# Attention with scores, maxima and values in TensorE tiles of 64 rows by 32 columns

## The chip, the cores and the metric

The kernel runs on one core of one Trainium2 chip. The metric is the device time of one execution in microseconds (us); less is better. Engines are named as in the profile: PE is TensorE (matmuls; PEld its weight loads), DVE is VectorE, ACT is ScalarE, POOL is GpSimd, SP is SyncE, which issues most DMAs.

## The reference

A transformer block on one sequence of 2048 rows and 512 columns, in float32: layer norm, attention with 32 heads of 16 columns, an output projection and a residual, then layer norm, a feed-forward part of width 1792 with SiLU, and a residual.

```python
def _A_ref(x, wqkv, wo):
    qkv = (x @ wqkv) split into q, k, v      # 32 heads of 16 columns
    scores = einsum("bhqd,bhkd->bhqk", q, k) * 16 ** -0.5
    o = einsum("bhqk,bhkd->bhqd", softmax(scores), v)
    return o @ wo
def _B_ref(x, w1, w2):
    return silu(x @ w1) @ w2
h = x + _A_ref(layernorm(x), A_wqkv, A_wo)
return h + _B_ref(layernorm(h), B_w1, B_w2)
```

## The kernel before, in words

**Stages.** A prelude normalizes and transposes the rows and projects q, k and v. Then come 32 *items* of attention; an item is four heads (two pairs, `HEADS`, line 55) by one block of 512 queries, so that eight items make a query block. After each of the first three query blocks the feed-forward part of that block runs as a stage of its own (`finish_block`, line 1104; `mlp`, line 1041), in the middle of the loop over groups; the last one runs at the end (`finish_last`, line 1121).

**Groups.** An item has 16 *groups* of 128 keys; the loop over the 512 groups starts at line 1244. Each group does three things for TensorE:

- *Scores* (`scores`, line 451): for each of the four heads a matmul with 128 keys as the stationary operand and 512 queries moving, contraction over 64 rows (48 of data and 16 that carry the maximum of each query), float16. The two heads of a pair lie in rows 0 to 63 and 64 to 127 of `ks` and `qs` (`64 * j`), so that scores of different `j` use different halves of TensorE's rows. ScalarE takes the exponential of the 128 by 512 result from PSUM into a float32 tile `pt` (line 460).
- *Maxima* (`maximum`, line 273) of a later item: a matmul with 128 queries stationary and 512 keys moving, over 48 rows, and on VectorE a maximum over the 512 (line 289). `one_max` (line 393) picks one of the half that is asked for. How many a group does is set by `maxima` (line 1221) from what is due; in the attention stretches it is three in nearly every group and two in the third group of an item (`JOINT`, line 1236). More are done in the prelude and in the feed-forward stages.
- *Values* (`values`, line 815) of the group two before (`LAG`): four float32 matmuls over all 128 keys, one for each head, with the 17 columns of `va` (16 of v and one of ones) stationary and `pt` moving. Head `k` writes PSUM rows `32 * k` on, so that the four use four different quarters of TensorE's columns. They add up over the 16 groups of the item in one PSUM bank, `pv`.

**Order.** All engines run their work in the order in which the program states it (`keep_in_program_order`). In a group the four scores come in turn with the maxima, each maximum on the other half of the rows than the score before it (lines 1287 to 1300); then what else is due (transposed maxima of an item, `place_max`, line 326; output projection, `output`, line 1087); then the four value products (line 1312).

**Banks.** PSUM has eight banks of 128 by 512 float32. In attention, four serve the scores in turn (`st`), three the maxima (`sm`), one is `pv` (lines 802 to 804).

**Item's end.** After the item's last values, `finish_item` (line 833) copies `pv` into the tile `pvs` (VectorE; ScalarE for items 8, 16 and 24, `FIRSTS`), and DMAs carry sums and values on. The last item has its two head pairs one after the other, the first ended by `finish_part` (line 862). In items 8, 16 and 24 the last groups also hold the output projection and the layer norm of the query block before, whose products take banks from `st`.

Of the kernel before, what the change touches and what calls it, by code (L numbers as in the profile page):

```python
# [10 lines left out]
F32 = mybir.dt.float32  # L11
# [4 lines left out]
ALU = mybir.AluOpType  # L16
# [4 lines left out]
P = 128  # L21
# [4 lines left out]
DH = 16  # L26
# [4 lines left out]
KC = S // P  # L31
# [16 lines left out]
LAG = 2  # L48
# [40 lines left out]
def attention_mlp_kernel(ctx: ExitStack, tc: tile.TileContext, x, wqkv, wo, w1, w2, out):  # L89
    nc = tc.nc  # L90
    x = x.flatten_outer_dims()
# [3 lines left out]
    def mm(*a, **k):  # L95
        tc.keep_in_program_order(nc.tensor.matmul(*a, **k))  # L96
# [12 lines left out]
    def act(fn, *a, **k):  # L109
        pin(getattr(nc.scalar, fn)(*a, **k))  # L110

    def dve(fn, *a, **k):
        pin(getattr(nc.vector, fn)(*a, **k))  # L113
# [115 lines left out]
    ks, qs = [None] * RING, [None] * RING  # L229
# [3 lines left out]
    va = vpool.tile([P, KC, H, DH + 1], F32, name="va")  # L233
# [36 lines left out]

    mx, left = {}, {}

    def maximum(i, kb, qt, a, j, n):

        piece = piece_of(i, a)
        width = 1 if i == LAST else 2
        if piece not in mx:
            mx[piece] = small.tile([P, 64], F32, name="mx", bufs=RING + 1)[:, :32 * width].rearrange(
                "p (j a q k) -> p j a q k", j=2, a=width, k=4)
            left[piece] = 32 * width  # L280
        heads = (0, 1) if j is None else (j,)
        for m, h in enumerate(heads):
            mm(space[:, n + m, :], qs[i % RING][64 * h:64 * h + 48, a, qt * P:qt * P + P],
               ks[i % RING][64 * h:64 * h + 48, a, kb * 512:kb * 512 + 512], start=True, stop=True)
        of = mx[piece][:, :, a % width, qt, kb]
        if j is None:
            pin(nc.vector.tensor_reduce(of, space[:, n:n + 2, :], axis=AX.X, op=ALU.max))  # L287
        else:
            pin(nc.vector.tensor_reduce(of[:, j:j + 1], space[:, n, :], axis=AX.X, op=ALU.max))  # L289
# [59 lines left out]
    at = {"item": 0, "done": 0, "half": 0, "step": 0, "due": 0, "attention": False, "group": None, "ready": 0, "next": 0, "blocks": True}  # L349
    agenda, late = {}, {}  # L350

    def soon(steps, fn, *a):
# [459 lines left out]
    wo_l = cpool.tile([P, DC, D], F16, name="wo_l")  # L812
    hth = cpool.tile([P, DC, 512], F16, name="hth")
    htl = cpool.tile([P, DC, 512], F16, name="htl")
    def values(g):
        i, c = divmod(g, KC)
        n = KC if i < LAST else HALF
        for k in range(4):
            a, j, keys = head(g, k)
            mm(pv[32 * k:32 * k + DH + 1, :], va[:, keys, 4 * (i % 8) + 2 * a + j, :], pts.pop((g, k)),  # L820
               start=c % n == 0, stop=c % n == n - 1)
        if c == KC - 1:
            finish_item(i)
        elif c % n == n - 1:
            finish_part()

    def place(i, k):

# [1 line left out]
        r = (4 * i + 2 * a + j) % 8 * 16  # L830
        return slice(r, r + 16)

    def finish_item(i):

        b, u = divmod(i, 8)
        pvs = bp.tile([P, 512], F32, name="pvs", bufs=1)
        if i == LAST:
            act("copy", pvs[:, :256], pv[:, :256])
            dve("tensor_copy", pvs[:, 256:], pv[:, 256:])
        elif i in FIRSTS:  # L840
            act("copy", pvs, pv)
        else:
            dve("tensor_copy", pvs, pv)
        if i == LAST:
            last.append(pvs)
            return
        dma(dn[i], pvs.rearrange("(k r) n -> k r n", r=32)[:, DH, :])
        for k in range(4):
            dma(ot[b % 2][place(i, k), :, u // 2, :], pvs[32 * k:32 * k + 16, :].rearrange("d (t n) -> d t n", n=P))

        steps = (1, 4, 5, 7) if u == 7 else (2, 6, 8, 10)
        for n, fn in zip(steps, (sums, invert, spread, divide) if u % 2 else (sums, invert, spread)):
            soon(n, fn, i)
        if i == ITEMS - 2:
            soon(10, divide_half)
            soon(12, split_half)
# [2 lines left out]

    def finish_part():
        pvs = bp.tile([P, 512], F32, name="pvs", bufs=1)
        dve("tensor_copy", pvs, pv)
# [176 lines left out]
    def mlp(b):  # L1041
# [18 lines left out]
                singles(2)  # L1060

        gates = []
        lay_out(st=range(4))
        for f in range(FC):
            tick()
            next_weights()
# [37 lines left out]
    def finish_block(b, pending):  # L1104

        act("activation", small.tile([P, 1], F32, name="sw"), ident[:, :1], AF.Silu)
        load_weights("w1", 4)
        for g in pending:
            values(g)
        mlp(b)  # L1110

# [9 lines left out]
    def finish_last(pending):  # L1121
        b = NB - 1
        for g in pending:
            values(g)
# [119 lines left out]
    for g in range(groups):  # L1244
# [35 lines left out]
                    load_weights("w1", f)  # L1280
                load_weights("w2", 0)
        if g == 1:
            dve("memset", pv, 0.0)
        at["group"] = g
        n = maxima(g)

        half = 1 - head(g, g % 2)[1]
        j = next_item()
        more = len(todo[j, half]) - len(todo[j, 1 - half]) if j < ITEMS else 0
        beside = range(n)  # L1290
        if n == 3 and more < 0:
            beside = range(1, 4)
        if n == 2 and more > 0:
            beside = 0, 2
        for m in range(4):
            k = m ^ (g % 2)
            if (g, k) not in pts:
                scores(g, k)
            if m in beside:
                one_max(1 - head(g, k)[1])  # L1300
        if found_at["step"] < at["step"]:
            finish_rest()
        for j in late.pop(at["step"], ()):
# [43 lines left out]
```

## Time and profile before

| | |
|---|---|
| device time, median of 3 runs (lowest to highest) | 1611.66 us (1611.49 to 1613.15) |
| profiled execution: its own time | 1613.29 us |
| profiled execution: span of the records | 1611.5 us, 28300 instructions |
| granted TensorE clock | 1.0 |
| value products (`ps<-pt,va`) | 4096 matmul records, mean 598 ns |
| scores (`ps<-qs,ks`) | 2048, mean 379 ns |
| maxima (`ps<-ks,qs`) | 2048, mean 380 ns |
| exponentials (`pt<-ps` on ACT) | 2048, mean 631 ns |

A line of a group reads: line of the kernel, engine, operation, output and inputs by the program's names, shapes, count, then busy time in us, mean ns of one, and idle time of the engine just before them with what ended it. Of a matmul, `64*128` ahead of the shape is the part of the array that it uses: 64 rows by 128 columns. Instructions of one engine overlap in the records (a matmul's or an exponential's mean is longer than the distance to the next one), so the distance between starts tells the pace. A line of the view in order of time begins with start and length in us and ends with the count of instructions merged in it. A line of busy time by stretch has the stretch, its length, and for PE, PEld, DVE, ACT and POOL the busy us with the number of instructions, then clock, DMA share and GB/s. Nearly all matmuls carry line 96 and all VectorE operations but reductions line 113, those of helpers, so groups are told apart by tile names.

### The profile page before, as it was taken

The page shows a single profiled execution, that of the slowest core. Times are in us where ns is not written, and L with a number is a line of the kernel's source. Part 1 is how long each engine was busy: PE and PEld are TensorE (multiplying, and loading weights), DVE is VectorE, ACT ScalarE, POOL GpSimd, SP SyncE. Part 2 cuts the span into 40 slices and gives each one's busy share as a digit, 9 for nine tenths or more (in the row PEclk, how much of TensorE's full clock was granted, in tenths as well). Part 3 has the DMA queues.
Part 4 walks back from the last instruction along what each step waited for, and adds up shares of the span by engine and source line. Part 5 has one row for each costly group of instructions (what it writes and reads, how often), then busy time and mean ns, then how long its engine had stood idle before and what let it go on. Part 6 is the DMA issues. An engine that isn't in the chain of part 4 may idle for free.

```text
span 1611.5 us, 28300 instructions
## 1 busy us (share of the span) xinstructions
PE 1590.8 (99%) x10553; PEld 477.9 (30%) x10553; DVE 1392.9 (86%) x2060; ACT 1210.3 (75%) x2387; POOL 456.4 (28%) x702
## 2 busy tenths in 40 slices
PE   9999999999999999999999999999999999999998
PEld 6433222222233322222233322222233322222253
DVE  7899999999989889999989889999976789999421
ACT  6545799999964179999964179999964089999732
POOL 4743544544326101211136101211126101111100
PEclk9999999999999999999999999999999999999999
DMA  5668533342322111121223211121123111100222
GB/s 194 181 162 234 139 85 90 110 140 85 101 63 99 60 52 33 37 60 33 51 73 99 60 52 33 38 59 33 50 75 108 50 52 38 33 11 22 73 85 72
DMA packets 100949, 125.89 MB, mean 78 GB/s; under 512 B 24144, under 2 KB 61072, under 8 KB 100812
## 3 DMA queue, kind: packets, MB, share of 16 engines
q1 hardware_dynamic: 96204, 115.71, 25.1%
q10 hardware_dynamic: 4608, 8.39, 1.9%
q8 instruction: 82, 1.34, 0.3%
q14 instruction: 55, 0.45, 0.1%
HBM read 93.45 MB, written 24.63 MB: 73 GB/s over the span
## 4 chain that ended last, share of the span: by engine, by line
PE 85%; DVE 6%; ACT 4%; DMA 2%; issue 1%; POOL 1%; SPq 1%; DVEq 0%; ACTq 0%; POOLq 0%
PE ps L96 84%; ACT pt L110 4%; DVE mx L289 2%; DVE mx L287 2%; PE ps L99 1%; DMA qd<-sh 1%; DVE ot L113 1%; SPq L116 1%; DMA qs<-mt 0%; DVE st L113 0%; DMA ks<-in_A_x_dram 0%; DVE htl L113 0%; DVE hx L113 0%; POOL ri L103 0%; DVE pvs L113 0%
## 5 line engine op out<-in xcount | busy, mean ns | idle before, releaser
L110 ACT ACTIVATE pt<-ps 128x512 f32<-128x512 f32 x2048 | 1011.3, 631 | 154.9 <-PE ps L96 153.4
L289 DVE TENSOR_REDUCE mx<-ps 128x1 f32<-128x512 f32 x1474 | 926.8, 683 | 44.9 <-PE ps L96 16.1
L96 PE MATMUL ps<-qs,ks 64*128 64x512 f16 x2048 | 533.6, 379 | 5.8 <-DMA qs<-mt 2.5
L96 PE MATMUL ps<-pt,va 128*17 128x512 f32 x4096 | 537.5, 598 | 0.6
L96 PE MATMUL ps<-ks,qs 48*128 48x512 f16 x2048 | 494.7, 380 | 1.8 <-DVE mx L287 1.8
L287 DVE TENSOR_REDUCE mx<-ps 128x2 f32<-128x1024 f32 x287 | 334.0, 1219 | 55.1 <-PE ps L96 54.1
L96 PEld LDWEIGHTS <-ks 64*128 64x128 f16 x2048 | 150.8, 95 | 553.0 <-issue 433.2
L103 POOL TENSOR_TENSOR ri<-rc,minus 128x16 f32<-128x16 f32 x31 | 90.7, 2925 | 294.8 <-DMA rc<-dn 294.8
L96 PE MATMUL ps<-w,gh 128*128 128x512 f16 x672 | 157.4, 380 | 0.5 <-ACT g L110 0.4
L96 PEld LDWEIGHTS <-qs 48*128 48x128 f16 x2048 | 125.1, 94 | 75.3 <-issue 61.9
L96 PE MATMUL ps<-hth,w 128*128 128x512 f16 (+1 forms) x472 | 132.9, 369 | 0.0
L96 PEld LDWEIGHTS ps<-pt,va 128*17 128x17 f32 x4096 | 68.9, 95 | 214.6 <-issue 201.1
L110 ACT ACTIVATE g<-ps,factors 128x512 f32<-128x512 f32 x56 | 38.6, 689 | 124.6 <-PE ps L96 102.9
L96 PEld LDWEIGHTS <-w 128*128 128x128 f16 x708 | 66.1, 98 | 79.1 <-issue 11.8
L103 POOL TENSOR_TENSOR mx<-mx 128x32 f32<-128x32 f32 x36 | 8.6, 239 | 281.8 <-DVE mx L289 216.6
L96 PEld LDWEIGHTS <-gh 128*128 128x128 f16 x672 | 61.1, 98 | 85.5 <-issue 19.8
L96 PE MATMUL ps<-htl,w 128*128 128x512 f16 (+1 forms) x236 | 83.9, 368 | 0.0
L103 POOL TENSOR_SCALAR nm<-nm 128x16 f32<-128x16 f32 (+1 forms) x51 | 12.9, 254 | 169.8 <-DVE nm L303 154.5
L110 ACT ACTIVATE ks<-ps 128x512 f32<-128x512 f32 x30 | 18.0, 599 | 50.3 <-PE ps L96 37.6
L113 DVE SCALAR_TENSOR_TENSOR gh<-g,factors,gh 128x512 f16<-128x512 f32 x14 | 10.5, 751 | 52.2 <-ACT gh L110 52.2
L103 POOL TENSOR_TENSOR sl<-ks,sh 128x512 f16<-128x512 f32 x30 | 35.3, 1178 | 52.9 <-ACT sh L110 38.5
L103 POOL TENSOR_TENSOR gh<-g,gh 128x512 f16<-128x512 f32 x42 | 48.5, 1154 | 3.5
(153 smaller groups left out, 983.5 us busy)
## 6 DMA issues: line engine op xcount, KB each, us to landing
ks<-kd SPq DMA_DIRECT2D x120, 192.0 KB
w<-w1d SPq DMA_DIRECT2D x56, 256.0 KB
w<-w2d SPq DMA_DIRECT2D x56, 256.0 KB
ks<-in_B_w_dram ACTq DMA_DIRECT2D x28, 256.0 KB
w<-in_B_w_dram SPq DMA_DIRECT2D x28, 256.0 KB
qs<-qd SPq DMA_DIRECT2D x128, 48.0 KB
kd<-sh SPq DMA_DIRECT2D x16, 256.0 KB
qd<-sh SPq DMA_DIRECT2D x16, 256.0 KB
```

Of the source, the lines that this page charges most:

```text
L96: tc.keep_in_program_order(nc.tensor.matmul(*a, **k))
L99: tc.keep_in_program_order(nc.tensor.transpose(*a))
L103: tc.keep_in_program_order(getattr(nc.gpsimd, op)(*a, **k))
L110: pin(getattr(nc.scalar, fn)(*a, **k))
L113: pin(getattr(nc.vector, fn)(*a, **k))
L116: pin(nc.sync.dma_start(*a))
L287: pin(nc.vector.tensor_reduce(of, space[:, n:n + 2, :], axis=AX.X, op=ALU.max))
L289: pin(nc.vector.tensor_reduce(of[:, j:j + 1], space[:, n, :], axis=AX.X, op=ALU.max))
```

## The change

In attention every matmul of a group gets one tile shape, 64 rows by 32 columns:

- `narrow` issues a score or a maximum as four matmuls, one for each 32 columns of the stationary operand; each writes 32 rows of the same PSUM bank. It does so while `at["narrow"]` is set, which is in attention and not in the feed-forward stages.
- `values` is split by keys: half 0 takes keys 0 to 63, half 1 keys 64 to 127, each with four matmuls over 64 rows and with a PSUM bank of its own (banks 6 and 7).
- A group is written as two halves. In the first: a score of the heads in rows 64 to 127, values of half 0 (rows 0 to 63), then one or two maxima and the second score, all of rows 64 to 127. In the second the row halves are exchanged.
- The banks in attention are three for scores, three for maxima, two for values; the feed-forward stages have theirs as before.
- At an item's end `copy_values` copies half 0's bank into `pvs` and adds half 1's bank to it on VectorE.

By the program's order TensorE has 50,126 matmuls and weight loads in place of 21,102; the other engines' work is that of before but for the additions into `pvs`. The diff, cut to its core:

```diff
+    def narrow(ps, w, x):
+        for t in range(4) if at["narrow"] else (None,):
+            cols = slice(None) if t is None else slice(32 * t, 32 * t + 32)
+            mm(ps[cols, :], w[:, cols], x, start=True, stop=True)
...
-            mm(space[:, n + m, :], qs[i % RING][64 * h:64 * h + 48, a, qt * P:qt * P + P],
-               ks[i % RING][64 * h:64 * h + 48, a, kb * 512:kb * 512 + 512], start=True, stop=True)
+            narrow(space[:, n + m, :], qs[i % RING][64 * h:64 * h + 48, a, qt * P:qt * P + P],
+                   ks[i % RING][64 * h:64 * h + 48, a, kb * 512:kb * 512 + 512])
...
-        mm(ps, ks[i % RING][64 * j:64 * j + 64, a, c * P:(c + 1) * P], qs[i % RING][64 * j:64 * j + 64, a, :],
-           start=True, stop=True)
+        narrow(ps, ks[i % RING][64 * j:64 * j + 64, a, c * P:(c + 1) * P], qs[i % RING][64 * j:64 * j + 64, a, :])
...
-    idle_bank, last_bank = banks["st"]
-    lay_out(st=range(4), sm=(4, 5, last_bank))
-    pv = space[:, idle_bank, :]
+    def lay_out_attention():
+        lay_out(st=range(3), sm=range(3, 6))
+        at["narrow"] = True
+    lay_out_attention()
+    pv = [space[:, 6 + n, :] for n in range(2)]
...
-    def values(g):
+    def values(g, half):
         i, c = divmod(g, KC)
         n = KC if i < LAST else HALF
+        rows = slice(64 * half, 64 * half + 64)
         for k in range(4):
             a, j, keys = head(g, k)
-            mm(pv[32 * k:32 * k + DH + 1, :], va[:, keys, 4 * (i % 8) + 2 * a + j, :], pts.pop((g, k)),
+            pt = pts.pop((g, k)) if half else pts[g, k]
+            mm(pv[half][32 * k:32 * k + DH + 1, :], va[rows, keys, 4 * (i % 8) + 2 * a + j, :], pt[rows],
                start=c % n == 0, stop=c % n == n - 1)
-        if c == KC - 1:
-            finish_item(i)
-        elif c % n == n - 1:
-            finish_part()
+        if c % n == n - 1:
+            copy_values(i, c == KC - 1, half)
...
+    def copy_values(i, whole, half):
+        if not half:
+            pvs = bp.tile([P, 512], F32, name="pvs", bufs=1)
+            sums_of.append(pvs)
+            if i in FIRSTS or i == LAST and whole:
+                act("copy", pvs, pv[0])
+            else:
+                dve("tensor_copy", pvs, pv[0])
+            return
+        pvs = sums_of.pop()
+        dve("tensor_tensor", pvs, pv[1], pvs, ALU.add)
+        if whole:
+            finish_item(i, pvs)
+        else:
+            finish_part(pvs)
...
+        beside = [n // 2, n // 2]
+        if n % 2:
+            beside[int(more > 0)] += 1
+        old = g - LAG >= 0 and not (g in marks or g - 1 in marks)
+        for half in range(2):
+            j = 1 - half
+            mine = [k for k in range(4) if head(g, k)[1] == j]
+            for m, k in enumerate(mine):
+                if (g, k) not in pts:
+                    scores(g, k)
+                if m == 0:
+                    if old:
+                        values(g - LAG, half)
+                    for _ in range(beside[j]):
+                        one_max(j)
...
-        if g - LAG >= 0 and not (g in marks or g - 1 in marks):
-            values(g - LAG)
```

More of the change, by code (lines that the diff above doesn't have):

```diff
@@ L348, in attention_mlp_kernel @@
     END = 64 * ITEMS
-    at = {"item": 0, "done": 0, "half": 0, "step": 0, "due": 0, "attention": False, "group": None, "ready": 0, "next": 0, "blocks": True}
+    at = {"item": 0, "done": 0, "half": 0, "step": 0, "due": 0, "attention": False, "narrow": False, "group": None, "ready": 0, "next": 0, "blocks": True}
     agenda, late = {}, {}
@@ L814, in attention_mlp_kernel @@
     htl = cpool.tile([P, DC, 512], F16, name="htl")
[L815 removed]
+    def values(g, half):
         i, c = divmod(g, KC)
         n = KC if i < LAST else HALF
+        rows = slice(64 * half, 64 * half + 64)
         for k in range(4):
             a, j, keys = head(g, k)
[L820 removed]
+            pt = pts.pop((g, k)) if half else pts[g, k]
+            mm(pv[half][32 * k:32 * k + DH + 1, :], va[rows, keys, 4 * (i % 8) + 2 * a + j, :], pt[rows],
                start=c % n == 0, stop=c % n == n - 1)
[L822 to L825 removed]
+        if c % n == n - 1:
+            copy_values(i, c == KC - 1, half)
+    sums_of = []
+    def copy_values(i, whole, half):
[13 more added lines that the diff above has]
+            finish_part(pvs)
     def place(i, k):
@@ L831, in place, with finish_item @@
         return slice(r, r + 16)
-    def finish_item(i):
+    def finish_item(i, pvs):
         b, u = divmod(i, 8)
[L836 to L843, printed above, removed]
         if i == LAST:
@@ L858, in attention_mlp_kernel, with finish_part @@
     rcs, last = {}, []
-    def finish_part():
-        pvs = bp.tile([P, 512], F32, name="pvs", bufs=1)
-        dve("tensor_copy", pvs, pv)
+    def finish_part(pvs):
         o_t = gp.tile([P, 4, P], F32, name="o_t", tag="oh")
@@ L1062, in mlp @@
         gates = []
-        lay_out(st=range(4))
+        lay_out(st=range(4), sm=(4, 5, 7))
+        at["narrow"] = False
         for f in range(FC):
@@ L1108, in finish_block @@
         for g in pending:
-            values(g)
+            for half in range(2):
+                values(g, half)
         mlp(b)
+        lay_out_attention()
     O = ot[(NB - 1) % 2]
@@ L1123, in finish_last @@
         for g in pending:
-            values(g)
+            for half in range(2):
+                values(g, half)
+        at["narrow"] = False
+        lay_out(st=range(4), sm=(4, 5, 7))
         o_t, pvs = last
@@ L1282, in attention_mlp_kernel @@
         if g == 1:
-            dve("memset", pv, 0.0)
+            for half in range(2):
+                dve("memset", pv[half], 0.0)
         at["group"] = g
         n = maxima(g)
-        half = 1 - head(g, g % 2)[1]
         j = next_item()
[L1289 to L1300, printed above, removed]
+        more = len(todo[j, 1]) - len(todo[j, 0]) if j < ITEMS else 0
+        beside = [n // 2, n // 2]
+        if n % 2:
+            beside[int(more > 0)] += 1
+        old = g - LAG >= 0 and not (g in marks or g - 1 in marks)
+        for half in range(2):
+            j = 1 - half
[8 more added lines that the diff above has]
+                        one_max(j)
         if found_at["step"] < at["step"]:
```

## The prediction

> **What bounds the kernel now.** I read the page first (busy shares, the chain of work that ended last, the costly groups), then busy time by stretch, then the groups of one steady stretch of attention, then the instructions there in order of time.
>
> ```profile
> PE 1590.8 (99%) x10553; PEld 477.9 (30%) x10553; DVE 1392.9 (86%) x2060; ACT 1210.3 (75%) x2387; POOL 456.4 (28%) x702
> ...
> PE 85%; DVE 6%; ACT 4%; DMA 2%; issue 1%; POOL 1%; SPq 1%; DVEq 0%; ACTq 0%; POOLq 0%
> ...
> L96 PE MATMUL ps<-pt,va 128*17 128x512 f32 x4096 | 537.5, 598 | 0.6
> ```
>
> By these lines TensorE is the limit, and a reader would expect whatever frees TensorE to pay. But the shares are averages over attention and the feed-forward stages, and matmul ends are modelled. So the steady attention stretch from 600 to 800 us, by itself:
>
> ```profile
> 600.00:800.00 200.00, 199.74 (x1527) 44.78 (x1520) 191.68 (x314) 199.76 (x407) 35.08 (x58) 1.00 0.17 42
> ```
>
> ```profile
> L110 ACT ACTIVATE pt<-ps 128x512 f32<-128x512 f32 x407 | 200.4, 627 | 0.2
> ```
>
> ```profile
> 432.06 21.75 ACT L110 ACTIVATE pt<-ps 128x512 f32<-128x512 f32 x44 [0.78 <-PE ps L96]
> ```
>
> Here TensorE, VectorE and ScalarE are all full, and ScalarE is fullest: its only work is the exponential of a score tile, with 0.2 us idle in 200. The third line shows its pace: 44 exponentials without a gap, the last one 0.6 us long, so (21.75 - 0.63) / 43 = 0.491 us from one to the next; 407 in 200 us give the same 0.491. A group has four scores, so it cannot take less than 4 x 0.491 = 1.96 us. TensorE's group, in order of time:
>
> ```profile
> 703.56 1.05 PE L96 MATMUL ps<-pt,va 128*17 128x512 f32 x8
> 704.55 0.39 PE L96 MATMUL ps<-qs,ks 64*128 64x512 f16 x1
> 704.55 0.39 PE L96 MATMUL ps<-ks,qs 48*128 48x512 f16 x1
> 704.77 0.38 PE L96 MATMUL ps<-qs,ks 64*128 64x512 f16 x2
> 705.00 0.38 PE L96 MATMUL ps<-ks,qs 48*128 48x512 f16 x1
> 705.22 0.38 PE L96 MATMUL ps<-qs,ks 64*128 64x512 f16 x1
> 705.52 0.23 PE L99 MATMUL ps<-ident_h,ns 128*32 128x128 f16 x1
> 705.53 1.05 PE L96 MATMUL ps<-pt,va 128*17 128x512 f32 x7
> ```
>
> The value products start at 703.56 and again at 705.53: 1.97 us. They hold TensorE 0.99 us (to 704.55); scores and maxima start 0.22 us apart on each half of the rows (704.55, 704.77, 705.00, 705.22). So TensorE's group is 1.96 us as well: **two engines with the same period**, and taking work off one of them leaves the other.
>
> **The change part by part.**
>
> *The tile shape.* Two shapes alternate now, 64 rows by 128 columns and 128 by 32, and each alternation costs TensorE a gap. Its price: in the block's finish three groups' value products run back to back.
>
> ```profile
> 841.26 2.77 PE L96 MATMUL ps<-pt,va 128*17 128x512 f32 x24
> ```
>
> ```profile
> 841.70 0.12 PEld L96 LDWEIGHTS ps<-pt,va 128*17 128x17 f32 x4 [0.31 <-issue]
> 842.13 0.12 PEld L96 LDWEIGHTS ps<-pt,va 128*17 128x17 f32 x4 [0.31 <-issue]
> ```
>
> Four matmuls per 0.43 us, two such passes for a group's values: 0.86 us. In the steady stretch they take 0.99, and four pairs of 0.22 take 0.98 where 0.88 would do. So the two switches cost 0.13 + 0.10 = 0.23 us a group. They go. A half of the rows then carries per group one half's values (0.86) and half of the scores and maxima: 299 maxima (row below) over 407 / 4 = 102 groups are 2.9 a group, so (4 + 2.9) / 2 x 0.22 = 0.76. Sum 1.62 us; in the written order the scores of one half wait for the values before them on the same rows, which makes it 2 x max(0.86, 0.22 x 4) = 1.76 where a half has two maxima. Either is below 1.96: **TensorE comes free by 0.2 to 0.34 us a group, and the exponentials set the same 1.96.** Gain in steady attention: none.
>
> It gains where ScalarE is idle. In the last six groups of items 8, 16 and 24 the output projection stands between groups:
>
> ```profile
> 457.11 2.07 ACT L110 ACTIVATE pt<-ps 128x512 f32<-128x512 f32 x4 [3.31 <-PE ps L96]
> 462.62 2.07 ACT L110 ACTIVATE pt<-ps 128x512 f32<-128x512 f32 x4 [2.93 <-PE ps L96]
> ```
>
> ScalarE waits about 3 us for TensorE in each. At most 18 x 0.23 = 4 us go; three score banks instead of four, of which the projection borrows one, take some back. I take **-3 us** (bounds -4 and +6: a score that waits for one VectorE operation of 0.7 us in half of the groups).
>
> *More instructions.* Per group 4 x 4 score and 2.9 x 4 maximum matmuls, and 16 for values (4096 / 512 = 8 now, twice that then): 44 matmuls and 44 weight loads, against 15 and 15. They must pass in 1.96 us, one in 22 ns. Nearest rows: eight weight loads with their matmuls begin within
>
> ```profile
> 701.49 0.13 PEld L96 LDWEIGHTS ps<-pt,va 128*17 128x17 f32 x8 [0.43 <-issue]
> ```
>
> 0.13 us (some 8 ns for one instruction, in a burst), and 1527 + 1520 instructions in the 200 us above (66 ns, sustained, and no demand for more). I take the burst, because there the array is ready and nothing else holds the instructions; cost 0, and the upper end is a rival.
>
> *One bank fewer for scores.* A bank is taken for 0.38 us of matmul and 0.63 of exponential, about 1.05 with what lies between. Three banks turn in 3 x 0.49 = 1.47 us, so a score may come 0.4 us late before ScalarE feels it; four banks gave 0.9. Cost in a regular group 0. The built program also gives three of four exponentials a second wait, on an old exponential; the copy of values below has seven waits and follows the maximum before it without idle time, so I take 0.
>
> *Values in two banks.* Each item's end now has a copy of bank 6 and an addition of bank 7, both on VectorE, in place of one copy.
>
> ```profile
> L289 DVE TENSOR_REDUCE mx<-ps 128x1 f32<-128x512 f32 x299 | 188.2, 684 | 8.3 <-PE ps L96 2.1
> L113 DVE COPY pvs<-ps 128x512 f32<-128x512 f32 x7 | 4.8, 680 | 0.0
> ```
>
> ```profile
> 702.31 2.52 DVE L289 TENSOR_REDUCE mx<-ps 128x1 f32<-128x512 f32 x4
> 704.74 0.68 DVE L113 COPY pvs<-ps 128x512 f32<-128x512 f32 x1
> 705.34 1.28 DVE L289 TENSOR_REDUCE mx<-ps 128x1 f32<-128x512 f32 x2
> ```
>
> ```profile
> L113 DVE TENSOR_TENSOR htl<-ps,hth 128x512 f16<-128x512 f32 x16 | 10.8, 681 | 2.0 <-ACT hth L110 2.0
> ```
>
> A maximum follows the next in (2.52 - 0.68) / 3 = 0.61 us, a copy in 0.60 (704.74 to 705.34); the addition is priced by the subtraction of like shape, 0.68, so 0.60 as well. VectorE's regular group is 2.9 x 0.60 = 1.76 of 1.96 us: 0.2 to spare. Follow the item's last group, time 0 at its first score. Half 0's values run from 0 to 1.05; the copy stands in VectorE's order right behind them and **ahead of this group's maxima**, which would have been ready at 0.6: it runs 1.1 to 1.7, two maxima to 2.9, the addition to 3.5, the third maximum to 4.1. The next group begins at 1.96; its first half's values find bank 6 free, its second half's values are due at 1.96 + 0.86 + about 0.1 = 2.9 and must wait for the addition, to 3.6: 0.7 us late, and behind them on TensorE wait a maximum and two scores. Against it stand TensorE's 0.2 us of slack and the scores' 0.4. So ScalarE loses between 0.1 and 0.7. Before, the same wait was there,
>
> ```profile
> PEld ps L96 <- DVE pvs L113: 1.9, 3, 0.7
> ```
>
> 0.7 us at the longest, and cost ScalarE nothing (no gap in the 44), covered by the fourth bank. In that next group also stands the transposition of the maxima (705.52 above): it is of the old shape, was next to values of the same shape, and now brings a switch there and back, 0.23 us, after the slack is spent. I take 0.3 + 0.2 = **0.5 us an item's end**, with bounds 0 and 1.0. VectorE copies values 29 times over the run, 28 of them at an item's end:
>
> ```profile
> L113 DVE COPY pvs<-ps 128x512 f32<-128x512 f32 x29 | 19.7, 681 | 6.3 <-PE ps L96 6.3
> ```
>
> 28 x 0.5 = **+14 us** (0 to +28). POOL's and SP's work is unchanged, one more small delay of the sums' DMAs included, which have ten groups to land. The last item's end adds at most 0.6 us (one addition).
>
> Sum: 14 - 3 = **+11 us**. The profiled execution took 1613.3 us (span 1611.5); the median of the three timed runs is 1611.7. On the profiled one that is 1624; on the median, **1623 us**.
>
> **The rivals.**
>
> *A. The slack covers the item's end (same or faster).* If three banks' 0.4 us and TensorE's 0.2 swallow the 0.7 us wait, nothing is lost there. For it: the wait of before cost nothing. Against it: the bank that covered it is gone. It decides below 0.6 us of lateness. Then -3 to -7 us (the projection groups, and the few short gaps of ScalarE before them): 1605 to 1609; with a tenth or two lost per end, 1609 to 1614.
>
> *B. Matmuls start strictly in written order.* Then the values' second pass, 0.43 us after the first, must have begun before a maximum of the other rows may start: first pass 0.43, two maxima and a score 0.66, so a half takes 1.09 and the other half 0.87: 1.96, with no slack and scores up to 0.4 late. About 0.1 us a group lost, over some 465 groups without projection: +46 us, 1660 or so. [...]
>
> *C. TensorE cannot take so many instructions, or the row halves do not run together.* The break-even is 22 ns an instruction. Half way between the two rows, about 35 ns, a group takes 88 x 0.035 = 3.1 us, and 465 x 1.1 = 530 us come on top: 2100 or so. If float32 values and float16 scores exclude each other, a group is 2 x 0.86 + 6.9 x 0.22 = 3.2 us, much the same. Against it: only the burst row. [...]
>
> **How the numbers follow.** About 0.2%, 3 us, is what a measurement of this kernel can tell from no change. Item's end loses as forecast, 1615 to 1645: 0.45. Rival A: 0.14 faster by more than 3 us, 0.17 within 3 us. Rival B, 1645 to 1700: 0.14. Rival C: 0.10. Together slower 0.69, same 0.17, faster 0.14. The range leaves out C, the upper part of B and a little of A: 1603 to 1675; the forecast's own range is 1615 to 1645.
>
> **What would show it.** In the steady stretch ScalarE stays at 0.49 us an exponential, while TensorE's groups show idle time before scores that ScalarE's banks release. Gaps of ScalarE, 0.3 to 1 us, stand two or three groups after each item's begin, and TensorE's waits there are put down to the addition into pvs. The gaps before the exponentials of the projection groups shrink from 3.3 and 2.9 us by about 0.2. I am wrong if exponentials come slower than 0.49 in regular groups (B or C), if ScalarE shows no gap at the items' ends (A), or if the gaps there come from something else than the addition and the transposition.

## The result, and the profile after

The kernel after takes **1703.77 us** (median of 3 runs, 1703.63 to 1704.31), against 1611.66 before: a ratio of **1.0569 (95%: 1.0545 to 1.0593)**, 92 us more. The prediction was 1623 us with a range of 1603 to 1675; the sign was right, the size was not. The profiled execution took 1704.31 us, its span 1702.5, its granted clock 1.0.

The page of the kernel after: busy shares, the chain of work that ended last, the exponentials.

```profile
PE 1668.3 (98%) x25065; PEld 667.8 (39%) x25065; DVE 1416.3 (83%) x2093; ACT 1244.6 (73%) x2387; POOL 457.9 (27%) x702
...
PE 68%; ACT 19%; DVE 7%; issue 4%; POOL 1%; DMA 1%; SPq 0%; DVEq 0%; ACTq 0%; POOLq 0%
...
L110 ACT ACTIVATE pt<-ps 128x512 f32<-128x512 f32 x2048 | 1047.2, 602 | 212.3 <-PE ps L96 204.3
```

TensorE shows 98%, against 99% before; the share says nothing of the loss. The chain does: PE 85% and ACT 4% before, now PE 68, ACT 19, DVE 7. More of the end is set by engines that hand work to each other in turn. Busy time by stretch, 600 to 800 us of the kernel after (PE, PEld, DVE, ACT, POOL, then clock):

```profile
600.00:800.00 200.00, 197.38 (x4013) 76.57 (x4016) 178.57 (x291) 186.68 (x368) 28.07 (x47) 1.00 0.17 44
```

368 exponentials where there were 407; no engine but TensorE is full, and TensorE's is a modelled fullness. Where is the time lost? ScalarE in order of time, in a stretch without an item's end:

```profile
648.07 4.06 ACT L110 ACTIVATE pt<-ps 128x512 f32<-128x512 f32 x8 [0.20 <-PE ps L96]
652.33 4.06 ACT L110 ACTIVATE pt<-ps 128x512 f32<-128x512 f32 x8 [0.20 <-PE ps L96]
656.59 4.06 ACT L110 ACTIVATE pt<-ps 128x512 f32<-128x512 f32 x8 [0.20 <-PE ps L96]
```

Eight exponentials, a gap, eight exponentials: two groups take 4.26 us and not 8 x 0.491 = 3.93. That is 0.165 us a group; with some 480 regular groups (512 less 18 with projection and those at the begin, at the blocks' ends and at the items' ends) 79 of the 92 us. The starts of all exponentials agree: in 26 of the 32 items (all but 8, 16, 24 and the one ahead of each), groups 5 to 16 of an item take 0.166 us more than before on average. **The loss is in steady attention, where the prediction had none.**

Why does it repeat every *two* groups? VectorE and TensorE in the same stretch:

```profile
654.15 0.69 DVE L295 TENSOR_REDUCE mx<-ps 128x1 f32<-128x512 f32 x1 [0.20 <-PE ps L96]
655.12 0.69 DVE L295 TENSOR_REDUCE mx<-ps 128x1 f32<-128x512 f32 x1 [0.28 <-PE ps L96]
```

```profile
653.00 0.62 PE L96 MATMUL ps<-pt,va 64*17 64x512 f32 x4
653.20 0.40 PE L96 MATMUL ps<-ks,qs 48*32 48x512 f16 x4
653.44 0.61 PE L96 MATMUL ps<-pt,va 64*17 64x512 f32 x4
...
653.97 0.62 PE L96 MATMUL ps<-pt,va 64*17 64x512 f32 x4
654.17 0.61 PE L96 MATMUL ps<-ks,qs 48*32 48x512 f16 x6
654.41 0.59 PE L96 MATMUL ps<-pt,va 64*17 64x512 f32 x1
654.41 0.38 PE L96 MATMUL ps<-ks,qs 48*32 48x512 f16 x2
654.42 0.60 PE L96 MATMUL ps<-pt,va 64*17 64x512 f32 x3
```

Look at the maximum whose matmuls start at 653.20. They are through at 653.60, but VectorE, idle for 0.20 us, takes it only at 654.15. What ended just before is the values' second pass: 653.44 + 0.61 = 654.05. The same at 655.12: own matmuls from 654.17, second pass through at 654.42 + 0.60 = 655.02. So VectorE starts 0.10 us after the end of *other* matmuls, written earlier and running on the other half of the rows. It is no accident of two lines: of the 77 maxima between 600 and 800 us ahead of which VectorE was idle over 0.1 us, all 77 start 95 to 102 ns after the end of a second pass of values, and 539 to 928 ns after the end of the maximum's own matmuls (starts less ends of the trace's records). Ends of matmuls are modelled, but the trace also holds the times at which TensorE raises the semaphore (the counter by which it tells another engine that work is done) that VectorE waits for: 654.12 and 655.10 for these two maxima, 23 or 24 ns ahead of VectorE's start in all 77 cases. So it is TensorE's report that is late, not VectorE.

My theory (theory 1), **order of reports**: TensorE reports a block of matmuls as done only when every block written before it is done. A maximum or score behind values waits for their second pass, about 1.05 us after the values' start, even though it ran beside them. The rest of the loop, from the exponential at 652.33 to that at 656.59:

```profile
655.39 0.61 PE L96 MATMUL ps<-pt,va 64*17 64x512 f32 x4
655.87 0.40 PE L96 MATMUL ps<-ks,qs 48*32 48x512 f16 x4
655.96 0.53 PE L96 MATMUL ps<-qs,ks 64*32 64x512 f16 x8
```

Third exponential of the eight through at 652.33 + 2 x 0.49 + 0.61 = 653.92; its bank goes to a score, values start behind it at 653.97; their second pass is through at 655.02; the maximum behind them is reduced from 655.12 to 655.81; a later maximum, which needs that bank, starts at 655.87; a score behind it on the same rows comes 0.22 later and its exponential at 656.59. In parts: 1.59 + 0.05 + 1.05 + 0.10 + 0.69 + 0.06 + 0.72 = 4.26 us, every engine waiting in turn. The parts follow one another, so their sum had to be the period; that each begins 0.05 to 0.10 us behind the end of what it waits for is what speaks for a loop, and the experiments below shorten single links of it. It should close once in two groups because the third maximum changes sides from group to group: the halves have 1, 2, 2, 1 maxima, and only where two halves of two meet does VectorE fall behind by three banks.

The rivals: **order of starts** (theory 2, rival B of the prediction: no later matmul may start before the values' second pass has begun), **too many instructions** (theory 3, rival C in a mild form: 88 in 2.13 us is what TensorE takes), and **the items' ends** (theory 4, the prediction's own term, only larger).

### The profile page after: what moved, and what is told of

The parts are those of the page before. It is cut to its first block, busy times and chain, and to the rows that moved or that the text cites. A ratio compares the mean times of both kernels' runs of the same rounds, so it can differ in the third digit from the quotient of the medians.

```text
span 1702.5 us, 59027 instructions
## 1 busy us (share of the span) xinstructions
PE 1668.3 (98%) x25065; PEld 667.8 (39%) x25065; DVE 1416.3 (83%) x2093; ACT 1244.6 (73%) x2387; POOL 457.9 (27%) x702
## 4 chain that ended last, share of the span: by engine, by line
PE 68%; ACT 19%; DVE 7%; issue 4%; POOL 1%; DMA 1%; SPq 0%; DVEq 0%; ACTq 0%; POOLq 0%
PE ps L96 67%; ACT pt L110 19%; DVE mx L293 2%; DVE mx L295 2%; PE ps L99 1%; DVE ot L113 1%; DVE pvs L113 1%; DVE htl L113 0%; DMA qs<-mt 0%; DVE st L113 0%; POOL rs L103 0%; DVE hx L113 0%; POOL oh L103 0%; SPq L116 0%; DMA ks<-in_A_x_dram 0%
## 5 line engine op out<-in xcount | busy, mean ns | idle before, releaser
L110 ACT ACTIVATE pt<-ps 128x512 f32<-128x512 f32 x2048 | 1047.2, 602 | 212.3 <-PE ps L96 204.3
L96 PE MATMUL ps<-pt,va 64*17 64x512 f32 x8192 | 1004.2, 593 | 4.6 <-DVE pvs L113 3.4
L96 PE MATMUL ps<-qs,ks 64*32 64x512 f16 (+1 forms) x8096 | 726.4, 381 | 15.1 <-DVE htl L113 5.0
L96 PE MATMUL ps<-ks,qs 48*32 48x512 f16 (+1 forms) x6416 | 621.3, 379 | 2.4 <-DVE mx L293 1.0
L96 PEld LDWEIGHTS <-ks 64*32 64x32 f16 (+1 forms) x8096 | 251.9, 90 | 446.6 <-issue 379.2
L96 PEld LDWEIGHTS <-qs 48*32 48x32 f16 (+1 forms) x6416 | 225.9, 90 | 260.1 <-issue 213.9
L96 PEld LDWEIGHTS ps<-pt,va 64*17 64x17 f32 x8192 | 159.2, 92 | 36.6 <-DVE pvs L113 7.6
```

## The experiments

Each was timed in three rounds beside the kernel before, which gave 1611.4 to 1611.9 us.

### Runs of eight

```diff
-            beside[int(more > 0)] += 1
+            beside[g // 8 % 2] += 1
```

> Edit: the third maximum of a group goes to the same rows for eight groups before it changes sides; in the change it changes sides from group to group, so that the halves have 1, 2, 2, 1 maxima. Nothing else changes. Theory 1 (order of reports): TensorE reports a block of matmuls as done only when every block written before it is done, so a maximum behind a values product is reported at the end of the values' second pass; where two halves of two maxima follow each other, a maximum then waits for VectorE to give back one of three banks, a score stands behind it, and ScalarE idles 0.34 us in every two groups. With runs of eight the two halves of two meet once in sixteen groups: about 70 of the 79 us lost in regular groups come back, 1704 - 70 = 1634 us (1622 to 1650), and the exponentials of regular groups are 0.49 us apart. Theory 2 (order of starts, rival B of the prediction): a half of two maxima costs 1.09 us wherever it stands, so 1690 to 1704. Theory 3 (too many instructions): their number is the same, 1701 to 1707. Theory 4 (the items' ends make the whole loss): 1701 to 1707.

Measured: **1656.96 us** (ratio to before 1.0280, 1.0262 to 1.0297), 47 us less than the change. The number of instructions, the items' ends and the halves of two maxima are all still there; only that two of them rarely meet is new. Theories 3 and 4 fall, and 2 in this form. But 1657 is 7 us over theory 1's own range. ScalarE in runs_of_eight:

```profile
669.71 19.07 ACT L110 ACTIVATE pt<-ps 128x512 f32<-128x512 f32 x38
```

No gap that the view would break the line at, yet (19.07 - 0.60) / 37 = 0.499 us an exponential and not 0.491: some 32 ns a group, about 15 us in all, which theory 1 as I had put it did not have. More of it below.

### Values first

```diff
-                if (g, k) not in pts:
-                    scores(g, k)
-                if m == 0:
-                    if old:
-                        values(g - LAG, half)
+                if m == 0 and old:
+                    values(g - LAG, half)
+                if (g, k) not in pts:
+                    scores(g, k)
+                if m == 0:
```

> Edit: in each half the four value products stand ahead of the first score instead of behind it. Theory 1 (order of reports): now all of a half, its first score too, is reported only at the end of the values' second pass, about 1.05 us after the values' start; the scores come later, two at a time, and three score banks carry less of that: 20 to 45 us more than the change, 1724 to 1750. Theory 2 (order of starts): nothing of the half may start before the values' second pass has begun, 0.43 us: a half takes 0.43 + 4 x 0.22 = 1.3 us and a group 2.4 to 2.6, so 1830 or more. Theory 3 (too many instructions): 1701 to 1707. If neither starts nor reports are held in order, the half is no worse than in the change, 1704 or less.

Measured: **1734.36 us** (1.0757, 1.0739 to 1.0775). Theory 1's 1724 to 1750; theory 2 would have needed 1830, theory 3 no change. The timeline of TensorE in values_first has starts that theory 2 forbids:

```profile
701.64 0.61 PE L96 MATMUL ps<-pt,va 64*17 64x512 f32 x4
701.91 0.40 PE L96 MATMUL ps<-qs,ks 64*32 64x512 f16 x4
702.07 0.61 PE L96 MATMUL ps<-pt,va 64*17 64x512 f32 x4
```

The score behind the values starts at 701.91, between their first pass (701.64) and their second (702.07). Starts are not held back by the second pass; reports are, in the change's 77 of 77 maxima.

### A shorter maximum

```diff
-            ...tensor_reduce(of[:, j:j + 1], space[:, n, :], ...)
+            ...tensor_reduce(of[:, j:j + 1], space[:, n, :256] if at["narrow"] else space[:, n, :], ...)
```

> Edit: in attention VectorE takes the maximum over 256 of a block's 512 scores (it leaves out half of the keys from the maxima; the matmuls stay). Theory 1 (order of reports): one maximum's time on VectorE stands in the loop of two groups, 4.26 us; half the columns take 0.25 to 0.3 us off it, which brings it to about the 3.93 us of eight exponentials: 1625 to 1650. Theory 2 (order of starts): VectorE is not in its loop, 1695 to 1704. Theory 3 (too many instructions): 1701 to 1707. Theory 4 (items' ends): the copy and the addition wait less for maxima, 1690 to 1700.

Measured: **1637.89 us** (1.0161, 1.0144 to 1.0178), 66 us less. TensorE's work is untouched, so it wasn't TensorE's rate that set the pace, and one VectorE instruction stands in the loop. Groups of short_maximum, 600 to 800 us:

```profile
L110 ACT ACTIVATE pt<-ps 128x512 f32<-128x512 f32 x400 | 200.2, 603 | 0.8 <-ACT pt L110 0.4
...
L295 DVE TENSOR_REDUCE mx<-ps 128x1 f32<-128x256 f32 x293 | 115.1, 421 | 75.3 <-PE ps L96 75.0
```

The maximum took 421 ns in place of 683: 0.26 us, twice the 66 / 480 = 0.14 that come back in a group, as a term that stands once in a loop of two groups should. VectorE now has 75 us to spare, and the maxima still come late: all 181 ahead of which it was idle over 0.1 us start 95 to 102 ns after the end of a second pass of values, as in the change.

### Narrow parts alone, on the kernel before

```diff
-            mm(space[:, n + m, :], qs[i % RING][64 * h:64 * h + 48, a, qt * P:qt * P + P],
-               ks[i % RING][64 * h:64 * h + 48, a, kb * 512:kb * 512 + 512], start=True, stop=True)
+            narrow(space[:, n + m, :], qs[i % RING][64 * h:64 * h + 48, a, qt * P:qt * P + P],
+                   ks[i % RING][64 * h:64 * h + 48, a, kb * 512:kb * 512 + 512])
...
-        mm(ps, ks[i % RING][64 * j:64 * j + 64, a, c * P:(c + 1) * P], qs[i % RING][64 * j:64 * j + 64, a, :],
-           start=True, stop=True)
+        narrow(ps, ks[i % RING][64 * j:64 * j + 64, a, c * P:(c + 1) * P], qs[i % RING][64 * j:64 * j + 64, a, :])
```

> Edit, on the kernel before: scores and maxima in four parts of 32 columns, as in the change, and nothing else: values over 128 rows in one bank, four banks for scores, the old order. 36 matmuls and 36 weight loads a group against 15 and 15. Theories 1, 2 and 4: parts of 32 columns cost nothing by themselves, 1612 us, within 8. Theory 3 (too many instructions): the group of the change has 88 instructions in 2.13 us, 24 ns each; if that is what TensorE can take, 72 need 1.75 us beside two changes of shape, and the kernel is slower than before by more than 10 us, above 1625.

Measured: **1627.52 us** (1.0093, 1.0076 to 1.0110): 16 us, twice the 8 that I allowed and by the letter theory 3's outcome. The value products of a group start, in the kernel before and in narrow_alone:

```profile
621.01 1.05 PE L96 MATMUL ps<-pt,va 128*17 128x512 f32 x8
...
622.97 1.05 PE L96 MATMUL ps<-pt,va 128*17 128x512 f32 x8
...
624.93 1.05 PE L96 MATMUL ps<-pt,va 128*17 128x512 f32 x8
```

```profile
621.28 1.05 PE L96 MATMUL ps<-pt,va 128*17 128x512 f32 x8
...
623.28 1.05 PE L96 MATMUL ps<-pt,va 128*17 128x512 f32 x8
...
625.26 0.62 PE L96 MATMUL ps<-pt,va 128*17 128x512 f32 x4
```

1.96 and 1.96 us against 2.00 and 1.98. Parts of 32 columns cost TensorE about 0.03 us a group, 512 x 0.03 = 15 us, where it has no time to spare. That is a price of its own, a sixth of what the change lost, and it does not bring theory 3 back: runs_of_eight and short_maximum pass the same instructions as the change in 47 and 66 us less. In the change's layout it lies hidden: with the same parts, eight_score_between below runs a regular group in 1.96 us.

### One pass

```diff
-            mm(..., va[rows, keys, 4 * (i % 8) + 2 * a + j, :], pt[rows],
+            mm(..., high(va[rows, keys, 4 * (i % 8) + 2 * a + j, :]), high(pt[rows]),
```

`high` is a view of the upper 16 bits of each float32 number as bfloat16.

> Edit, on the change: the value products read the upper 16 bits of each float32 number of both operands as bfloat16 (less exact values), so that TensorE needs one pass for them and not two. Theory 1 (order of reports): a values product is over about 0.4 us after its start and not 1.05, so the maxima and scores behind it are reported when they are done themselves; all the loss of regular groups goes, some 79 us, the items' ends stay with about 15: 1625 us (1615 to 1635); VectorE's maxima start 0.1 us after their own matmuls. Theory 4 (the items' ends make the loss): 1690 or more.

Measured: **1624.58 us** (1.0077, 1.0060 to 1.0094), as theory 1 had it. TensorE and VectorE in one_pass:

```profile
661.41 0.40 PE L97 MATMUL ps<-pt,va 64*17 64x512 bf16 x4
661.61 0.61 PE L97 MATMUL ps<-ks,qs 48*32 48x512 f16 x8
```

```profile
662.05 2.48 DVE L296 TENSOR_REDUCE mx<-ps 128x1 f32<-128x512 f32 x4 [0.24 <-PE ps L97]
```

The maximum starts at 661.61, takes 0.40, and VectorE has it at 662.05. Of 44 maxima that VectorE waited for between 600 and 800 us, all 44 start 40 to 50 ns after the end of the maxima's own matmuls. The granted clock of this kernel was 0.97 to 0.98, with stretches at 0.50 that hold part of the 13 us over the kernel before; where it was 1.00, busy time by stretch shows 406 exponentials in 200 us, the pace of the kernel before:

```profile
200.00:400.00 200.00, 188.90 (x3633) 73.10 (x3633) 190.19 (x318) 199.04 (x406) 95.07 (x135) 1.00 0.36 104
```

Without the second pass the steady loss is gone. One pass also takes work off TensorE (4096 records of value matmuls, where the change has 8192), so this run alone does not part the late report from the load; runs_of_eight, short_maximum and eight_score_between, which keep TensorE's work, do.

### The addition at an item's end left out

```diff
         pvs = sums_of.pop()
-        dve("tensor_tensor", pvs, pv[1], pvs, ALU.add)
```

> Edit, on runs_of_eight (1657): the addition of the second bank at an item's end is left out (the output lacks half of the keys), the copy of the first bank stays. By the prediction's own sum the copy, the addition and the wait behind it cost 0.3 us an item's end and the transposition 0.2, so 28 x 0.3 = 8 us go: 1649 (1643 to 1653). If the ends lose their time to the transposition or to the score banks alone, 1655 to 1658.

Measured: **1649.23 us** (1.0233, 1.0216 to 1.0250), 7.7 us less than runs_of_eight. On that kernel the prediction's price of the addition and its wait was right, and it is less than a tenth of what the change lost.

### The score between the maxima

```diff
-                if m == 0:
-                    if old:
-                        values(g - LAG, half)
-                    for _ in range(beside[j]):
-                        one_max(j)
+                if m == 0 and old:
+                    values(g - LAG, half)
+                for _ in range(min(1, beside[j]) if m == 0 else max(0, beside[j] - 1)):
+                    one_max(j)
```

> Edit, on runs_of_eight (1657): a half's second score stands right behind the first maximum, and the second maximum behind that score. runs_of_eight still loses 35 ns in every group. My theory of it: a second loop of 2.0 us, per group: the exponential of a half's second score gives back its bank, the first score of the next group takes it, the values stand behind that score, their second pass ends 1.07 us later, and only then are two maxima and the second score of that half reported, one after the other, the score about 0.08 us after the first maximum. With one maximum fewer ahead of it the score is reported sooner by 0.02 to 0.06 us, and 15 us or so come back: 1635 to 1648. If the 35 ns are an exponential's own second wait, or the bank of a maximum, nothing changes: 1654 to 1660.

Measured: **1637.88 us** (1.0162, 1.0145 to 1.0179), 19 us less, with the same work in another order of two blocks. ScalarE in eight_score_between:

```profile
663.96 18.23 ACT L110 ACTIVATE pt<-ps 128x512 f32<-128x512 f32 x37
```

(18.23 - 0.60) / 36 = 0.490 us: the regular group is back at the pace of the kernel before. It is the least that the change's layout reached with all its work and values in float32, and 26 us more than before. By the starts of the exponentials, the first four groups of an item lose 0.46 us together against the kernel before and the other twelve 0.23 (the same 26 items); which causes share this rest was not tried, but for the additions.

### The values' halves with wide scores

```diff
-        at["narrow"] = True
+        at["narrow"] = False
```

> Edit, on the change: scores and maxima in one piece of 128 columns again; the values stay in two halves of 64 rows by 32 columns with a bank each. It asks whether the one tile shape is needed. If work on the two halves of the rows runs side by side only in one shape, a group takes 2 x 0.86 for values, 6.9 x 0.22 for scores and maxima and a change of shape at each of its 8 to 10 borders, above 3.2 us: 2200 us or more. If shapes mix freely, the same loops as in the change: 1690 to 1710.

Measured: **2951.25 us** (2928.36 to 2973.86). A stretch of attention in halves_wide, TensorE in order of time, and busy time with the granted clock (1.00 in the first line, 0.50 in the second):

```profile
352.50 1.05 PE L96 MATMUL ps<-pt,va 64*17 64x512 f32 x8
353.49 0.39 PE L96 MATMUL ps<-ks,qs 48*128 48x512 f16 x1
353.49 0.60 PE L96 MATMUL ps<-qs,ks 64*128 64x512 f16 x2
354.02 1.05 PE L96 MATMUL ps<-pt,va 64*17 64x512 f32 x8
```

```profile
250.00:600.00 350.00, 350.00 (x2472) 61.99 (x2471) 218.00 (x338) 233.38 (x430) 96.14 (x133) 1.00 0.23 64
1000.00:1200.00 200.00, 200.00 (x765) 23.34 (x762) 66.42 (x103) 71.84 (x132) 11.55 (x21) 0.50 0.06 13
```

Values, then the rest, then values: at full clock a half with one maximum takes 1.52 us, and 430 exponentials in 350 us make 3.26 us a group, as expected for no overlap (above 3.2). Values do not lie beside scores or maxima, though the rows are different ones. Two long stretches at half clock, where a group takes 6.1 us, bring the time beyond the 2200 us. The scores start 0.99 us behind the values (353.49 and 352.50), the same as in the kernel before (704.55 and 703.56), where values lie over all rows. halves_wide differs from the change in the shape of scores and maxima alone, so in this kernel the one tile shape is what lets the halves run together at all (2.13 us a group in place of 3.26), and the change's group of 2.13 us is no failure of that. Why two shapes wait for each other, no run shows.

### Maxima of half a bank, with three and with four score banks

```diff
+    def room(n):
+        if n < 8:
+            return space[:, n, :]
+        return space[:, n // 2, 256 * (n % 2):256 * (n % 2) + 256]
...
-        lay_out(st=range(3), sm=range(3, 6))
+        lay_out(st=range(3), sm=range(8, 12))
```

A maximum's matmuls and its reduction use `room(n)` and 256 keys; half_maxima_four differs by `st=range(4)` alone.

> Edit, on the change: each maximum of attention is taken over 256 keys of 512, matmuls and VectorE alike (half of the keys are left out of the maxima), so that a maximum needs half a bank; four of them in banks 4 and 5, three banks for scores as in the change, bank 3 lies idle. It is the control of the next run. Of the two loops that the order of reports makes, the one through VectorE should be gone as in short_maximum (1638), the one through the three score banks, 2.0 us a group, should stay: 1628 to 1642, with 20 to 40 ns lost in nearly every regular group.

> Edit, on half_maxima_three: bank 3 goes to the scores, four banks instead of three, and nothing else changes. If the loop of 2.0 us a group runs through the score banks (exponential, bank, first score of the next group, values behind it, their second pass, report), a fourth bank opens it: the 20 to 40 ns a group go, 10 to 18 us less than half_maxima_three, and the items' ends, covered again, lose less too: 1612 to 1626. If the bank has no part in it, as the prediction had it with its slack of 0.4 us, the two are within 3 us of each other.

Measured: 1956.73 us (1.2158, 1.2125 to 1.2190) and 1947.89 us (1.2079, 1.2054 to 1.2104). Both expectations fail, and the comparison does not tell what it was made for. VectorE and TensorE in half_maxima_three:

```profile
735.94 0.42 DVE L306 TENSOR_REDUCE mx<-ps 128x1 f32<-128x256 f32 x1 [0.70 <-PE ps L96]
```

```profile
734.73 0.29 PE L96 MATMUL ps<-ks,qs 48*32 48x256 f16 x4
734.80 1.04 PE L96 MATMUL ps<-pt,va 64*17 64x512 f32 x8
736.42 0.29 PE L96 MATMUL ps<-ks,qs 48*32 48x256 f16 x4 [0.58 <-DVE mx L306]
```

The maximum of 734.73 is reduced at 735.94, 0.10 us after the values behind which it stands are through (734.80 + 1.04), and only when that reduction has ended, at 736.36, does the next maximum start. So halves of a bank were not two places: the next maximum waited for its neighbour's reduction, and in this stretch the late report stands in that wait. The start follows VectorE's semaphore (`[0.58 <-DVE mx L306]`), so this is a wait that the built program contains, not a conflict that the trace shows in the chip. What a fourth score bank is worth by itself stays open; its 8.8 us here are those of another bound.

## Why the prediction was wrong, point by point

- *Both engines full, 1.96 us each:* right, and the base of all that follows.
- *The switches go, TensorE's group becomes 1.62 to 1.76 us, the exponentials set the same 1.96: gain and loss nothing.* **This step failed.** The load was not the mistake: eight_score_between, with the same matmuls, runs at 0.49 us an exponential (how far below 1.96 us TensorE's group could come, no run shows). The step counted when TensorE's blocks *run* and took that as when other engines *get* them. In the kernel before, values lie over all rows, scores and maxima start 0.99 us behind the values' start (704.55 and 703.56), and the two times lie together: the nine maxima that VectorE waited for between 600 and 800 us start 68 or 69 ns after the end of their own matmuls. In the change work runs beside values and is handed over when they are through: VectorE gets a maximum 539 to 928 ns after its own matmuls (0.55 us for that of 653.20), and two groups take 4.26 us. One step, 79 of 92 us.
- *Rival B, matmuls start strictly in written order, 1660 us, 0.14:* it named the place, the values' second pass, and fell short of the size. Its rule is not what the trace shows: the maximum of 653.20 starts ahead of the second pass at 653.44, and values_first measured 1734 where it needs 1830. Starts even leave the written order. The line of 655.96 holds two scores; the one written first is the second to start, at 656.08, 0.22 behind the maximum on its rows, and yet TensorE reports it first, at 656.50, and the other at 656.56. This occurs 39 times between 600 and 800 us. So across the halves of the rows the starts are not in written order; the reports are, in these 39 pairs and in the 77 of 77 maxima, which VectorE has 95 to 102 ns after the end of the values' second pass.
- *One bank fewer for scores, a slack of 0.4 us, cost 0:* wrong, since a bank was taken to be held 1.05 us; behind values it waits for their report as well: the score of 653.47 is through at 653.87 and is reported at 654.18, 0.13 us after the second pass of the values ahead of it (654.05), while the one of 652.98, written ahead of its half's values, is through at 653.38 and is reported at 653.40. That the remaining 32 ns a group went when a score was reported sooner, by 19 us of gain, fits; no run shows the bank alone. The copy at 704.74 has one wait in its trace and not seven, but the second wait of three in four exponentials does cost nothing: eight_score_between has it too, at 0.490 us.
- *More instructions, cost 0, rival C 2100:* 0 in the change is right, 88 in 2.13 us pass, 24 ns each, or 48 ns for each of the 44 matmuls; the 35 ns an instruction of rival C were the author's estimate between two rows, and no run shows them. On the kernel before, whose TensorE is busy for 199.74 of the 200 us, the parts cost 16 us (narrow_alone). The row that the cost was read from was misread: the eight weight loads of 701.49 do begin together (0.13 us is the time to the end of the last), but only four of the eight matmuls begin with them, the other four at 701.93.
- *Projection groups, -3 (-4 to +6):* the wrong sign, within its bounds. The last regular run of exponentials and the last copy of that stage, before and after:

```profile
439.44 14.36 ACT L110 ACTIVATE pt<-ps 128x512 f32<-128x512 f32 x29
...
477.54 0.62 ACT L110 CAST hth<-ps 128x512 f16<-128x512 f32 x1
```

```profile
473.76 3.57 ACT L110 ACTIVATE pt<-ps 128x512 f32<-128x512 f32 x7 [0.20 <-PE ps L96]
...
480.24 0.60 ACT L110 ACTIVATE pt<-ps 128x512 f32<-128x512 f32 x1 [2.91 <-PE ps L96]
481.07 1.64 ACT L110 ACTIVATE pt<-ps 128x512 f32<-128x512 f32 x3 [0.24 <-PE ps L96]
...
502.88 0.58 ACT L110 CAST hth<-ps 128x512 f16<-128x512 f32 x1
```

  From 453.80 to 478.16 before, 24.4 us; from 477.33 to 503.46 after, 26.1: +1.8 us here, and 2.1 and 1.7 in the two other such stages, over 5 in all. The first gap does shrink (3.31 to 2.91, 2.93 to 2.56 in the next group), and a new one of 0.24 behind the first exponential takes most of it back; what is lost is lost in the last three groups.
- *Items' ends, +14:* within its bounds, about half the size. 92 less 79 less 5 leaves 8; by the starts of the exponentials, the first four groups of an item together lose 0.22 us more than four of its regular groups, 6 us over 28 items. In runs_of_eight the addition alone is worth 7.7 of the predicted 8. The transposition's 0.2 us was not tried.
- *What would show it wrong:* "if exponentials come slower than 0.49 in regular groups (B or C)". They do, 0.53 on average, and from a cause that is neither B nor C.

## What to carry to other kernels

When two matmul streams share TensorE, draw two timelines for each block: when it runs, and when its consumer may have it, which in this kernel was no sooner than the end of every block written before it. Here the long product delayed the short ones written behind it (a maximum reached VectorE 539 to 928 ns after its own matmuls), and with a ring of banks on each side that closed a loop of 4.26 us in two groups; what helped is a shorter long product (one pass: 79 us), a shorter step in the loop (66 us) or an order in which the blocks that are needed soonest stand first and bursts do not meet (47 and 19 us). Look for a gap that repeats with a fixed period and follow its chain back over one period; then shorten one link and see whether the period shrinks by as much, as the shorter maximum showed.

## What the runs showed of the hardware that was not expected

- In the change, a maximum on one half of the rows that VectorE waited for reached it only when earlier matmuls on the other half were through: 95 to 102 ns after these in 77 of 77 cases between 600 and 800 us, 539 to 928 ns after its own end. Reports that were held back come 59 ns apart (654.12 and 654.18; 656.50 and 656.56). Whether TensorE holds the result or only the report is not told apart by any run here.
- The second pass of a float32 product did not hold back later starts (653.20 ahead of 653.44), but its end counted for later reports (654.05 ahead of 654.12). Scores on different halves of the rows started out of written order 39 times in 200 us, and were reported in it.
- Two tile shapes on different halves of the rows did not run side by side, in halves_wide: 3.26 us a group at a granted clock of 1.00. In that kernel the clock was 0.50 from 762 to 1493 us and again from 1626 to 2356, with TensorE shown as 100% busy (200.00 of 200 us from 1000 to 1200).
- Two halves of one bank were not independent places in this built program: a maximum waited for VectorE's reduction of the other half, 1957 us for maxima that are half as long, where 1638 was measured with whole banks.
